# A chunked state-space scan and two feed-forward layers on one core: the first decays' broadcast, idle products, and the order of issue changed

## The chip, the cores and the metric

The kernel runs on one core of a Trainium2 chip. The metric is the time on the device in microseconds: the median of three executions, 371.07 us before the change (371.06 to 371.11). TensorE does the matrix products, VectorE and ScalarE work on rows, GpSimd (POOL) does a few small things, and SyncE (SP) issues nearly all DMAs.

## The reference: what is computed

There are three stages, on 4 sequences of 768 tokens, with 8 heads of 32 channels each and a state of 16. All of it is float32. Stage 1 is a scan with decay in chunks:

```python
for c in range(nc):
    cum = np.cumsum(log_a[:, :, sl], axis=-1)
    L = np.exp(cum[:, :, :, None] - cum[:, :, None, :]) * causal
    CB = np.einsum('bhin,bhjn->bhij', Cc, Bc)
    y_intra = np.einsum('bhij,bhjd->bhid', CB * L, xc)
    y_inter = np.einsum('bhin,bhnd->bhid', Cc, state) * np.exp(cum)[:, :, :, None]
    y[:, :, sl] = y_intra + y_inter
    state = decay_full * state + sum_j(B_j x_j * decay_from_j)
```

Stages 2 and 3 are feed-forward layers over 256 channels with 1024 hidden ones. Between them the tokens of a sequence are mixed through a matrix of rank 32:

```python
x = x + relu(layer_norm(x) * g @ w_ch1) @ w_ch2
u = x + (x.T @ U @ V).T
out = u + relu(u @ w21) @ w22
```

## The kernel before

**Tiles.** The tokens are worked in 24 chunks of 128, six to a sequence, in groups of 256 and 512 tokens (`GROUPS`). A chunk goes through the same steps: its operands are loaded (`xb`, `stk`), the decays are spread over all partitions (`bc`), a scan makes the decay matrix `lt` (line 707, VectorE), products make `cb` (lines 718, 723, TensorE), `mult` joins both into `mm` (lines 733, 736, VectorE), `bw` weights the input for the state (line 754), `sps` and `gst` carry the state on (lines 813, 831), and `yps` is the chunk's output (lines 771 to 798, TensorE). [...] It is also transposed (`tps`, line 888) for mean and variance.

**Feed-forward layers.** A group of tokens has eight hidden slices `f`. For each there is a group of six first products (`mm1`, `hps`, line 960), a high part by ScalarE (`hh`, line 967), a low part by VectorE (`hl`, line 971) and a group of second products (`mm2`, `acc`, lines 985 and 991). The first products of the first layer need centred weights: `pc` (line 401) multiplies each piece of `w1` by a centring matrix, and a closing product with `negi` (line 414) leaves the low part. The weights arrive as words of 64 bits; two ScalarE steps and a VectorE merge (`w`, line 381) make float32 of them, in three staging buffers (`raw`).

**The first four chunks' decays** don't go through DRAM. Eight rows are loaded into `r` (line 633), clipped, split into a high and a low part `rh` (lines 662, 272), and TensorE spreads them with a selection matrix `sel`:

```python
P.matmul(p, pair["sel"][:2 * ROWS, k, :], pair["h"][:, j, :], start=(j == 0), stop=(j == 1))
```

**The order.** The program is a list of items with an engine, a cost, predecessors and a due time. `Plan.issue` replays them by its own costs and at each step emits the item that is due first, so that the tables `FIRST`, `SHIFT`, `WARM` and the cost functions set the order on each engine. Every engine then runs its own list in order. `FIRST` lists items that go ahead of everything; `STAY` favours staying with feed-forward products once there (a bonus in the due time); `NEAR` lets an item wait a little for a better one. At most eight DMAs are under way, and SP's queue is in order.

**Idle products.** Where the plan sees TensorE without work early on, it emits products of zeros on zeros into a bank that nobody reads (`filler`, line 1145, tile `dummy`), as long as the next item is more than `WARM[3]` away. They wait for the tile `zero` (line 320), which VectorE sets first of all.

## Time and profile before

| | |
|---|---|
| median of three executions | 371.07 us |
| the profiled execution | 372.6 us |
| its span, first to last instruction | 370.7 us |
| mean granted clock of TensorE | 0.982 of full |
| PE busy | 361.2 us, 97% |
| DVE busy | 235.5 us, 64% |
| ACT busy | 169.9 us, 46% |
| POOL busy | 32.4 us, 9% |
| DMA bytes | 40.16 MB, mean 108 GB/s |

The page gives each engine's busy time and, below, its share in 40 slices of the span, in tenths (9 is 90% or more). [...] The view in order of time has start, length, engine, line, tile written from tiles read, and in brackets the idle time before it with what ended it. A product in float32 shows as two instructions. Lengths of products overlap, so the time that one costs is the distance between starts. The chain of waits follows the last instruction back to what released it, step by step.

### The profile page before, as it was taken

The page shows a single profiled execution, that of the slowest core. Times are in us where ns is not written, and L with a number is a line of the kernel's source. Part 1 is how long each engine was busy: PE and PEld are TensorE (multiplying, and loading weights), DVE is VectorE, ACT ScalarE, POOL GpSimd, SP SyncE. Part 2 cuts the span into 40 slices and gives each one's busy share as a digit, 9 for nine tenths or more (in the row PEclk, how much of TensorE's full clock was granted, in tenths as well). Part 3 has the DMA queues.
Part 4 walks back from the last instruction along what each step waited for, and adds up shares of the span by engine and source line. Part 5 has one row for each costly group of instructions (what it writes and reads, how often), then busy time and mean ns, then how long its engine had stood idle before and what let it go on. Part 6 is the DMA issues. An engine that isn't in the chain of part 4 may idle for free.

```text
span 370.7 us, 8298 instructions
## 1 busy us (share of the span) xinstructions
PE 361.2 (97%) x3297; PEld 306.8 (83%) x3297; DVE 235.5 (64%) x516; ACT 169.9 (46%) x475; POOL 32.4 (9%) x44
## 2 busy tenths in 40 slices
PE   6999899999999999999999999999999999999996
PEld 4677789879887789899887789989986789898895
DVE  5699889998627864884556794567626742343242
ACT  5488567886614651522424641233415552242231
POOL 3452744000002000000000000000000000000000
PEclk8599899999999999999999999999999999999999
DMA  7938636652002576780131505243011100000010
GB/s 216 275 110 281 173 108 204 205 167 87 6 17 88 202 293 197 221 282 1 57 94 44 198 3 184 71 150 129 9 35 44 38 21 0 2 0 30 1 58 28
DMA packets 29308, 40.16 MB, mean 108 GB/s; under 512 B 3806, under 2 KB 19214, under 8 KB 29270
## 3 DMA queue, kind: packets, MB, share of 16 engines
q1 hardware_dynamic: 28982, 39.46, 33.5%
q8 instruction: 26, 0.43, 0.5%
q10 hardware_dynamic: 288, 0.17, 0.2%
q14 instruction: 12, 0.10, 0.1%
HBM read 31.67 MB, written 7.95 MB: 107 GB/s over the span
## 4 chain that ended last, share of the span: by engine, by line
PE 84%; DVE 9%; DMA 4%; issue 1%; ACT 1%; SPq 0%; DVEq 0%
PE hps L960 33%; PE acc L991 19%; PE acc L985 15%; PE pc L401 2%; PE yps L777 2%; DMA xt<-in_xb 2%; PE cb L723 2%; PE ups L1072 1%; DMA raw<-in_w 1%; PE tps L888 1%; DVE hl L971 1%; DVE w L381 1%; PE yps L771 1%; PE cb L718 1%; PE yps L789 1%
## 5 line engine op out<-in xcount | busy, mean ns | idle before, releaser
L971 DVE SCALAR_TENSOR_TENSOR hl<-hps,hh 128x256 fp32r<-128x256 f32 (+1 forms) x128 | 70.5, 552 | 90.5 <-ACT hh L967 90.3
L967 ACT ACTIVATE hh<-hps 128x256 fp32r<-128x256 f32 (+1 forms) x128 | 62.7, 491 | 140.4 <-PE hps L960 137.7
L960 PE MATMUL hps<-yhl,w 128*128 128x512 f32 (+1 forms) x384 | 80.1, 344 | 0.1
L960 PE MATMUL hps<-uhl,w 128*128 128x256 f32 (+1 forms) x384 | 77.6, 338 | 0.0
L991 PE MATMUL acc<-hh,w 128*128 128x512 f32 (+1 forms) x256 | 74.4, 343 | 0.0
L985 PE MATMUL acc<-w,hh 128*128 128x256 f32 x384 | 73.5, 287 | 0.4 <-DVE w L272 0.4
L960 PEld LDWEIGHTS hps<-yhl,w 128*128 128x128 f32 x384 | 60.1, 193 | 8.5 <-issue 1.0
L960 PEld LDWEIGHTS hps<-uhl,w 128*128 128x128 f32 x384 | 60.8, 190 | 7.6 <-DVE uhl L272 0.3
L985 PEld LDWEIGHTS acc<-w,hh 128*128 128x128 f32 x384 | 62.2, 192 | 4.5 <-issue 1.0
L985 PE MATMUL acc<-w,hl 128*128 128x256 f32 x192 | 54.8, 285 | 0.0
L991 PEld LDWEIGHTS acc<-hh,w 128*128 128x128 f32 x256 | 46.0, 189 | 7.4 <-issue 1.2
L991 PE MATMUL acc<-hl,w 128*128 128x512 f32 (+1 forms) x128 | 43.1, 337 | 0.0
L707 DVE TENSOR_TENSOR_SCAN lt<-lt,eye 128x512 f32<-128x512 f32 x32 | 38.9, 1217 | 5.9 <-DMA lt<-arows 5.9
L985 PEld LDWEIGHTS acc<-w,hl 128*128 128x128 f32 x192 | 37.0, 193 | 0.0
L681 POOL TENSOR_SCALAR stp<-stp,parity 128x256 f32<-128x256 f32 x20 | 24.8, 1250 | 15.0 <-DMA stp<-in_cbT 14.9
L991 PEld LDWEIGHTS acc<-hl,w 128*128 128x128 f32 x128 | 24.2, 189 | 2.2
L736 DVE TENSOR_TENSOR mm<-cb,lt 128x512 f32<-128x512 f32 x24 | 15.6, 682 | 3.5 <-PE cb L723 3.5
L372 ACT ACTIVATE w<-raw 128x512 f32<-128x512 f32 (+2 forms) x19 | 12.2, 642 | 9.1 <-DVE w L272 3.7
L376 ACT ACTIVATE raw<-raw,half 128x512 int32<-128x512 uint16 (+2 forms) x19 | 13.9, 734 | 0.0
L269 ACT ACTIVATE yhl<-yps 128x128 fp32r<-128x128 f32 x48 | 11.1, 278 | 5.9 <-PE yps L777 3.0
L272 DVE TENSOR_TENSOR yhl<-yps,yhl 128x128 fp32r<-128x128 f32 x48 | 11.5, 282 | 3.0 <-ACT yhl L269 1.6
L269 ACT ACTIVATE yt<-tps 128x256 f32<-128x256 f32 x24 | 9.1, 378 | 9.2 <-PE tps L888 9.0
(110 smaller groups left out, 372.1 us busy)
## 6 DMA issues: line engine op xcount, KB each, us to landing
raw<-in_w SPq DMA_DIRECT2D x16, 512.0 KB, 5.4
lt<-arows SPq DMA_DIRECT2D x12, 512.0 KB, 4.6
stk<-st SPq DMA_DIRECT2D x48, 96.0 KB, 2.5
st<-sh SPq DMA_DIRECT2D x8, 384.0 KB, 6.8
xt<-in_xb SPq DMA_DIRECT2D x14, 192.0 KB, 3.6
lt<-arows SPq DMA_DIRECT2D x16, 128.0 KB, 4.0
out<-u SPq DMA_DIRECT2D x8, 256.0 KB, 2.1
xt<-in_xb SPq DMA_DIRECT2D x20, 96.0 KB, 3.4
```

Source lines behind the costliest of these rows:

```text
L269: A.activation(out=out, in_=in_, func=AF.Copy, **kw)
L272: eng.tensor_tensor(out=out, in0=in0, in1=in1, op=ALU.subtract)
L372: A.activation(out=cell["t"], in_=words(1).bitcast(F32), func=AF.Prelu, scale=2.0 ** -112, alpha=-2.0 ** 32)
L376: A.activation(out=words(0), in_=cell["r"][:rows, :2 * n].bitcast(U16).rearrange("p (n w) -> p n w", w=4)[:, :, 1], func=AF.Identity, scal ...
L681: eng.tensor_scalar(out=t[:, 2 + i], in0=t[:, 1], scalar1=m, scalar2=None, op0=ALU.mult)
L707: V.tensor_tensor_scan(t, pair[k] if k < ROWS else t, eye, 0.0, op0=ALU.mult, op1=ALU.add)
L736: V.tensor_tensor(out=mm_[k][:, s_], in0=cbp[k, hf], in1=lt[k][:, s_], op=ALU.mult)
L960: P.matmul(p[:, :n], w[:, k, fs], x[:, k, :], start=(i == 0), stop=(i == 5))
L967: A.activation(out=hh[:, :n], in_=hps[l, key, f][:, :n], func=AF.Relu)
L971: V.scalar_tensor_tensor(out=hl[:, :n], in0=hps[l, key, f][:, :n], scalar=0.0, in1=f32(hh[:, :n]), op0=ALU.max, op1=ALU.subtract)
L985: P.matmul(p, x[:, t * C:(t + 1) * C], w[:, f, :], start=(f == 0 and i == 0 and t % 2 == 0), stop=(f == NF - 1 and i == 2), skip_group_che ...
L991: P.matmul(accs[l, key][d][:, :n], w[:, f, ds_], x[:, :n], start=(f == 0 and i == 0), stop=(f == NF - 1 and i == 2))
```

## The change

It has four parts, and the new constants of the planner go with them.

- **Broadcast.** The tile `rh` has 128 rows, not 8. VectorE sets it to zero first (`bcz`, 1024 columns), then the eight rows are written as before, and the product contracts over all 128 rows of `sel` and `rh`.
- **Idle products.** Once a gap is found, idle products are emitted until the plan's time is 0.2 us past the moment at which the next item can start; before, until it was nearer than 0.3 us. There are 57 of them, not 29.
- **First loads.** `FIRST` names the first chunks' operands ahead of the weights. `cst0` goes to the end of that list, and so stands behind `ra` on ScalarE's queue.
- **Order.** New costs, shifts, `STAY` 2.65 for 1.24, `NEAR` 0.03 for 0, and an item that follows on its own engine counts no latency.

```diff
--- before.py
+++ after.py
@@ -22,14 +22,14 @@
 NF = DFF // 128
 GROUPS = ((0, 256), (256, 512))
 
-WARM = (1.2, 6.0, 28, 0.3)
+WARM = (1.1, 3.8, 28, 0.3)
 EARLIEST = {'warm': 30.0}
 NS = (2, 2, 1, 1)
 FINE = sum(n == 2 for n in NS)
 PARTS = ((0, 2), (2, NC))
 
-FIRST = [('bc0', 0), (('w1', 0, 0), 'ld'), 'cst', (('w1', 0, 1), 'ld'), ('stk', 2), 'rows', ('xb', 0), 'cst0',
-         ('stk', 0), ('ra', 0, 0), ('sel', 0), ('bcl', 0), (('w2', 0, 0), 'ld'), ('ra', 0, 2)]
+FIRST = [('bc0', 0), ('sel', 0), ('stk', 0), ('xb', 0), ('bcl', 0), ('stk', 2), 'cst', (('w1', 0, 0), 'ld'),
+         ('ra', 0, 0), 'rows', (('w1', 0, 1), 'ld'), (('w2', 0, 0), 'ld'), ('ra', 0, 2), 'cst0']
 
 ACTQ = ['cst0', ('ra', 0, 0)]
 
@@ -42,23 +42,23 @@
          "000 001 010 101 011 020 100 111 021 110 030 121 031 120 131 130".split()]
 
 
-LAT, PER, T0, NEAR, SWITCH, STAY = 0.287, 1, -5.78, 0, 0.056, 1.24
+LAT, PER, T0, NEAR, SWITCH, STAY = 0.287, 1, -6.36, 0.03, 0.056, 2.65
 dve = lambda n: 0.065 + n / 960
 scn = lambda n: 0.06 + n / 480
 dve2 = lambda n: 0.065 + n / 1920
 mmr = lambda n: (n + 32) / 2400
 act = lambda n: 0.093 + n / 1200
 actp = lambda n: 0.051 + n / 1200
-pool_tt = lambda n: 0.0024 * n
-sp = lambda n, kb, run: (ISSUE * n, kb / 16 * (0.04 / run + 1 / 36))
+pool_tt = lambda n: 0.0043 * n
+sp = lambda n, kb, run: (ISSUE * n, kb / 16 * (0.045 / run + 1 / 31))
 BLOCK, FETCH = 256, 5.8
 ISSUE, FLIGHT, BEGIN = 0.52, 8, 0.75
-SP_FIRST, SP_LAST = 0.65, 0.92
+SP_FIRST, SP_LAST = 0.4, 0.8
 FIRST_NEAR = 2.0
 
 
 
-SHIFT = dict(zip("rows w0 w1 w2 ra0 ra chunk0 chunk".split(), [-96.3, -27.2, -54.91, 17.22, -39.9, -41.6, -51.31, -1.1]))
+SHIFT = dict(zip("rows w0 w1 w2 ra0 ra chunk0 chunk".split(), [-3.25, -6.22, -22.15, 12.19, -25.03, -114.94, -21.66, 2.83]))
 
 
 def kind(n):
@@ -181,7 +181,8 @@
             it = items[n]
             if eng == "PE":
                 now = max(free[eng], WARM[0])
-                while n != "dummy" and now < WARM[2] and t - now > WARM[3]:
+                gap = t - now > WARM[3]
+                while n != "dummy" and now < WARM[2] and gap and t + 0.2 > now:
                     self.filler()
                     step = dict(words=2, cost=0.109 if now > WARM[1] else 0.216)
                     now = max(now, self.fetched(step))
@@ -220,7 +221,7 @@
             it["fn"]()
             left -= 1
             for m in succ[n]:
-                at[m] = max(at[m], end)
+                at[m] = max(at[m], free[eng] if items[m]["eng"] == eng and not it["dma"] else end)
                 wait[m] -= 1
                 if not wait[m]:
                     ready.setdefault(items[m]["eng"], set()).add(m)
@@ -636,7 +637,7 @@
 
             p = pair[k] = ps_m.tile([128, 512], F32, tag="m", name="bcp")
             for j in range(2):
-                P.matmul(p, pair["sel"][:2 * ROWS, k, :], pair["h"][:, j, :], start=(j == 0), stop=(j == 1))
+                P.matmul(p, pair["sel"][:, k, :], pair["h"][:, j, :], start=(j == 0), stop=(j == 1))
 
         def bcast():
             lt[k] = att_p.tile([128, 1024], F32, tag="lt", name="lt", bufs=3)
@@ -647,7 +648,9 @@
             if k == 0:
                 pair["r"] = y_p.tile([2 * ROWS, 512], F32, tag="uhl0", name="r2")
                 pair["sel"] = y_p.tile([128, ROWS, C], F32R, tag="uhl1", name="selr")
-                pair["h"] = y_p.tile([2 * ROWS, 2, 512], F32R, tag="yhl1", name="rh")
+                pair["h"] = y_p.tile([128, 2, 512], F32R, tag="yhl1", name="rh")
+                ours = pair["h"][:2 * ROWS]
+                add(("bcz", k), "DVE", 1.0, lambda: V.memset(f32(pair["h"]), 0.0), due=-3e3)
                 sl_ = pair["sel"].rearrange("p k (i t) -> p (k i) t", i=2)
                 for j in range(0, ROWS, 2):
 
@@ -659,8 +662,8 @@
                 add(("bc1", k), "DVE", dve2(512), lambda: clip(pair["r"]), [("bc0", k)])
                 add(("bc2", k), "DVE", 0.07, lambda: V.memset(
                     pair["r"].rearrange("p (h i) -> p h i", i=w_)[:, :, 0:1], 0.0), [("bc1", k)])
-                add(("bch", k), "DVE", dve2(512), lambda: V.tensor_copy(pair["h"][:, 0, :], pair["r"]), [("bc2", k)])
-                add(("bcl", k), "DVE", dve(512), lambda: sub(V, pair["h"][:, 1, :], pair["r"], f32(pair["h"][:, 0, :])),
+                add(("bch", k), "DVE", dve2(512), lambda: V.tensor_copy(ours[:, 0, :], pair["r"]), [("bc2", k), ("bcz", k)])
+                add(("bcl", k), "DVE", dve(512), lambda: sub(V, ours[:, 1, :], pair["r"], f32(ours[:, 0, :])),
                     [("bch", k)])
             add(("bc", k), "PE", 0.46, bcast_first, [("bcl", 0), ("sel", k)], ring="m", words=4)
         else:
```

On TensorE at the start, where the first broadcasts (`bcp`, from `rh` and `selr`) stand, this is the end of the first 20 idle products and what follows before:

```order
L1145 MATMUL dummy<-zero 128x256
L639 MATMUL bcp<-rh,selr 128x512 x6
L401 MATMUL pc<-w_138,gd 128x256
L401 MATMUL pc<-w_138,gm 128x256 x2
L401 MATMUL pc<-w_138,gd 128x256
L639 MATMUL bcp<-rh,selr 128x512 x2
L1145 LDWEIGHTS zero
L1145 MATMUL dummy<-zero 128x256
```

And now, behind 23 idle products:

```order
L1148 MATMUL dummy<-zero 128x256
L640 MATMUL bcp<-rh,selr 128x512 x6
L721 MATMUL cb<-stp 64x256 x8
L640 MATMUL bcp<-rh,selr 128x512 x2
L1148 LDWEIGHTS zero
L1148 MATMUL dummy<-zero 128x256
```

The centring of the first weight piece (`pc`) is gone from between the broadcasts, and `cb` of the first two chunks stands there; 15 idle products follow.

On TensorE a little later, this is the stretch from the second centring to the first two chunks' outputs (`yps`) before:

```order
L401 MATMUL pc<-w_194,gd 128x256
L401 MATMUL pc<-w_194,gm 128x256 x2
L401 MATMUL pc<-w_194,gd 128x256
L813 MATMUL sps<-xt_93,bw 32x64 x8
L718 MATMUL cb<-stp 64x256 x8
L813 MATMUL sps<-xt_93,bw 32x64 x8
L414 MATMUL pc<-w_211,negi 128x512
L718 MATMUL cb<-stp 64x256 x8
L789 MATMUL yps<-rcb,gst 32x64 x8
L798 MATMUL yps<-mm,xt_93 32x64 x16
```

And now, from those outputs on, behind 13 more idle products:

```order
L792 MATMUL yps<-rcb,gst 32x64 x8
L801 MATMUL yps<-mm,xt_93 32x64 x16
L792 MATMUL yps<-rcb,gst 32x64 x16
L801 MATMUL yps<-mm,xt_93 32x64 x16
L891 MATMUL tps<-cst,yc 128x128 x2
L402 MATMUL pc<-w_260,gd 128x256
L402 MATMUL pc<-w_260,gm 128x256 x2
L402 MATMUL pc<-w_260,gd 128x256
L402 MATMUL pc<-w_362,gd 128x256
L402 MATMUL pc<-w_362,gm 128x256 x2
L402 MATMUL pc<-w_362,gd 128x256
```

Both chunks' outputs moved ahead of the first two centrings, which now follow each other. Behind them come four groups of first products (`hps`) in a row, where two stood alone before. Up to the first product of 512 columns the new order has all eight groups of first and eight of second products of the first token group, and five pairs of transposes; the order before has eight, six and four there. Over the whole program TensorE goes from feed-forward products to others 40 times, not 58; behind that first product of 512 columns 35 times, not 52.

On SP, the first DMAs before (`r` holds the first decays, `raw` a weight piece, `stp` and `xt` the chunks' operands):

```order
L254 DMA r_99<-in_a_rows 8x512
L254 DMA raw_112<-in_w 128x2x512
L254 DMA cst<-in_consts 128x256
L254 DMA raw_126<-in_w 128x2x512
L254 DMA stp<-in_cbT 128x256 x2
L254 DMA rows<-in_a_rows 88x256
L254 DMA xt_93<-in_xb 64x2x384 x2
L254 DMA stp<-in_cbT 128x256 x2
```

And now:

```order
L255 DMA r_99<-in_a_rows 8x512
L255 DMA stp<-in_cbT 128x256 x2
L255 DMA xt_93<-in_xb 64x2x384 x2
L255 DMA stp<-in_cbT 128x256 x2
L255 DMA cst<-in_consts 128x256
L255 DMA raw_170<-in_w 128x2x512
L255 DMA rows<-in_a_rows 88x256
L255 DMA raw_187<-in_w 128x2x512
L255 DMA raw_202<-in_w 128x2x512
```

The operands of the first chunks moved ahead of the first weight piece, and `rows` behind it.

## Rows read from the trace of the kernel before

**Rows 1.** The page's slices for PE, then stretches of the whole core.
```profile
PE   6999899999999999999999999999999999999996
...
5.00:10.00 5.00, 2.80 (x10) 1.95 (x9) 3.17 (x6) 2.64 (x5) 0.30 (x2) 0.72 1.05 297
...
15.00:20.00 5.00, 5.00 (x59) 3.46 (x57) 2.10 (x5) 2.82 (x6) 0.00 (x0) 0.76 0.57 153
40.00:50.00 10.00, 9.57 (x177) 8.80 (x178) 9.06 (x21) 7.15 (x26) 6.96 (x7) 0.83 0.42 120
50.00:60.00 10.00, 10.00 (x69) 8.35 (x69) 9.87 (x27) 6.12 (x13) 5.01 (x4) 1.00 0.61 174
```

**Rows 2.** TensorE in order of time, 0 to 20 us.
```profile
1.05 3.65 PE L1145 MATMUL dummy<-zero 128*128 128x256 bf16 x20 [1.05 <-DVE zero L320]
4.63 1.66 PE L639 MATMUL bcp<-rh,selr 8*128 8x512 f32 x6
8.48 1.22 PE L401 MATMUL pc<-w,gd 128*128 128x256 f32 x2 [2.20 <-DVE w L381]
```

**Rows 3.** The same stretches view, half a microsecond each: the granted clock.
```profile
7.00:7.50 0.50, 0.00 (x0) 0.00 (x0) 0.50 (x2) 0.50 (x2) 0.00 (x0) 0.66 1.07 379
...
17.00:17.50 0.50, 0.50 (x2) 0.39 (x2) 0.00 (x0) 0.00 (x0) 0.00 (x0) 0.60 0.81 272
```

**Rows 4.** The stretch 20 to 41, and a piece of the chain of waits.
```profile
20.00:41.00 21.00, 18.39 (x394) 13.94 (x394) 19.12 (x47) 15.54 (x47) 11.23 (x12) 1.00 0.77 219
...
32.74 6.43 DMA xt<-in_xb
```

**Rows 5.** TensorE in order of time, 46 to 52 us.
```profile
46.50 0.65 PE L789 MATMUL yps<-rcb,gst 32*32 32x64 f32 x32
...
47.46 0.51 PE L985 MATMUL acc<-w,hh 128*128 128x256 f32 x2
...
48.28 0.88 PE L960 MATMUL hps<-yhl,w 128*128 128x256 f32 x6
49.00 0.40 PE L985 MATMUL acc<-w,hh 128*128 128x256 f32 x2
...
49.72 0.88 PE L960 MATMUL hps<-yhl,w 128*128 128x256 f32 x6
50.52 1.09 PE L718 MATMUL cb<-stp 64*64 64x256 f32 x16
51.55 0.74 PE L960 MATMUL hps<-yhl,w 128*128 128x512 f32 x2
```

**Rows 6.** VectorE in order of time, 0 to 50 us.
```profile
0.82 0.17 DVE L320 MEMSET zero<- 128x128 f32 x1 [0.82 <-PEq L1188]
2.46 0.77 DVE L467 TENSOR_SCALAR r<-r 8x512 f32<-8x512 f32 x1 [1.47 <-DMA r<-in_a_rows]
3.29 0.07 DVE L660 MEMSET r<- 8x8 f32 x1
...
8.35 1.22 DVE L707 TENSOR_TENSOR_SCAN lt<-bcp,eye 128x512 f32<-128x512 f32 x1
...
43.58 0.55 DVE L467 TENSOR_SCALAR ra<-ra 128x768 f32<-128x768 f32 x1
```

**Rows 7.** TensorE in order of time, 22 to 26 us; last, pieces of the chain of waits.
```profile
22.93 0.50 PE L1145 MATMUL dummy<-zero 128*128 128x256 bf16 x3
23.27 0.38 PE L888 MATMUL tps<-cst,yc 128*128 128x128 f32 x2
23.81 0.70 PE L401 MATMUL pc<-w,gd 128*128 128x256 f32 x2 [0.16 <-DVE yhl L272]
...
25.64 0.38 PE L888 MATMUL tps<-cst,yc 128*128 128x128 f32 x2
...
19.49 0.36 PE sps L813 x16
19.85 0.42 PE pc L414
```

## The prediction

> **What bounds the kernel now.** I read the stretches first, then the clock, then TensorE's order of time, since only the engine that is never idle sets the end. TensorE is busy in nearly every slice of the span, and from 50 us on all of the time; VectorE is as full there (9.87 of 10 us) [rows 1]. So an end that comes earlier must come from the first 50 us, or from TensorE doing the same products in less time. In the first 50 us three things are lost. TensorE runs 20 idle products, then broadcast products that contract over 8 rows, and then stands 2.20 us for the first converted weights [rows 2]. The granted clock drops to half at about 7.2 us and is back at about 17.3 [rows 3]; between lie weight centring, broadcasts and six more idle products. VectorE meanwhile has only 2.10 us of work in 15 to 20 [rows 1]: the first chunks' products stand behind the weights. Between 20 and 41 TensorE is busy for 18.39 of 21 us and stands for 2.61; the longest of it ends a DMA on which the chain stood for 6.43 us, for the fifth chunk's `x` [rows 4]. Then the clock is lost again: its mean over 40 to 50 is 0.83 [rows 1], so 0.17 x 10 = 1.7 us are lost. The page's execution took 372.6 us with a span of 370.7; the median is 371.07, 1.5 below it. I take differences in the span and subtract them from the median.

> I compare at a **marker**: TensorE's first product of 512 columns, at 51.55 [rows 5]. Both orders have done there all eight first products of the first group, six chunks and all four centrings.

> **The start.** The new memset stands ahead of `zero`, for which the idle products wait. VectorE memsets take 0.07 us for 8 columns and 0.17 for 128 [rows 6], 0.83 ns a column, so 1024 columns take 0.92; at the rate of the clip of 768 columns in 0.55 [rows 6] it would be 0.73. I take 0.92, from the same operation. TensorE starts at 1.05 [rows 2] + 0.92 = 1.97. What else is queued behind the memset on VectorE loses nothing: the clip of the first rows waits for its DMA to 2.46 [rows 6]. The constants, now behind the first decays on ScalarE's queue, are wanted only for the selectors ahead of the first broadcast. [...]

> An idle product takes (23.27 - 22.93)/3 = 0.11 at full clock [rows 7], so 0.22 at half. The 20 idle products took from 1.05 to 4.63 [rows 2]; all at full clock would be 2.2 us, all at half 4.4, so some 12.5 ran at half and the clock rose near 3.8, after 2.7 us of them. The changed kernel will have run only 1.8 us of them at that time. That work alone doesn't bring it back at once is seen from 8.48 on, where TensorE went on without a gap and the clock came only at 17.3 [rows 2, 3]. I therefore expect the rise late, near the 7.15 us at which the clock changed before. The 23 idle products end at 1.97 + 23 x 0.22 = 7.0; with a rise at 3.8, 8 of them at half, at 5.4.

> **The broadcasts.** A product of 512 columns costs by columns: six took 1.66 with 8 rows [rows 2], and I price 128 rows the same, at nothing more. The rows that are added hold zeros. What they may give is the clock, since the clock fell just behind the 8-row products; after the rise nothing idles TensorE now, as idle products fill each gap.

> **The first chunks ahead of weights.** Before the first weight piece SP and ScalarE now load 16 + 128 + 37 + 512 + 384 = 1077 KB. At 297 GB/s [rows 1] from about 1.7 these are in by 5.4, and the weight of 512 KB (with 128 KB of constants) by 7.5, before its merge is due (13). VectorE needs the chunk's operands at 5 and later, so DMA hides here.

> TensorE's path, with full clock from 7.15: six broadcasts to 8.4; `cb` 1.05 to 9.5; two broadcasts to 9.9; 15 idle products to 11.6; both `sps`, 0.36 each, to 12.3; 13 idle products to 13.7; two chunks' outputs, 0.96 (46.50 to 47.46) and three quarters of it, to 15.5; transposes, 0.38, to 15.9; two centrings of 1.83 (23.81 to 25.64) to 19.6; transposes, two closing products of 0.42 and `cb` (50.52 to 51.55) to 21.8; four groups of first products in a row, 4 x 0.72 (48.28 to 49.00), to 24.7 [rows 5, 7]. VectorE can follow: its broadcast is there at 7.6, two scans of 1.22 to 10.0 [rows 6], `bw` to 10.5, in time for `sps`.

> From there to the marker stand: `sps` four times (1.4), six idle products (0.7), two centrings (3.7), two closing products (0.8), four chunks' outputs (3.8), four groups of first products (2.9), eight of second products at 0.72, 49.00 to 49.72 (5.8), two `cb` (2.1), three pairs of transposes (1.1): 22.3. Ten switches between the two kinds add 0.9 (below). The marker comes at 24.7 + 23.2 = 47.9, **3.65** earlier. VectorE bounds it from the other side: before, it was idle for 1.83 us in 5 to 10, 2.90 in 15 to 20 and 1.88 in 20 to 41 [rows 1, 4], 6.6 in all, and now for 1.2 while it waits for the broadcast. It can be 5.4 ahead, no more. Done by the marker are two more groups of second products (2 x 0.72) and a pair of transposes (0.38): **1.8** more, 5.45 with the 3.65, so that the two engines bound it alike.

> **Fewer switches.** A group of second products right after a chunk's output takes 0.82 (47.46 to 48.28), between first products 0.72; one of first products ahead of `cb` 0.80 (49.72 to 50.52) in place of 0.72 [rows 5]. Behind the marker TensorE leaves the FFN 35 times, not 52. 17 round trips at 0.18 are 3.1 us; nothing is the other bound, as transposes that lead into a mix may switch freely. I take half: **1.5**.

> **What such a chain leaves out** are waits not seen on paper. I charge half of the 2.61 us for which TensorE stood between 20 and 41 [rows 4]: **1.3**. Sum: 3.65 + 1.8 + 1.5 - 1.3 = 5.65, so 371.07 - 5.65 = **365.4**.

> **Rivals.** *Early rise.* The clock is full at 3.8 as before. The idle products end 1.6 earlier, of which VectorE lets TensorE keep 1.2 (its wait for the broadcast): 364.2. Against it stands the shorter run of products before that point.

> *Operands late further on.* The weight pieces need staging buffers that VectorE frees; loads behind them on SP wait too. If the hole of 39 us returns, it costs the other half of 2.61 and 1.7 of clock, 3.0: 368.4. For it: this very thing happened [rows 4]; against it: with the first operands ahead of the weights, the two first centrings no longer hold up chunks.

> *The clock isn't held.* If 128 zero-filled rows and idle products don't keep it, TensorE goes from 7 to about 17 at half again. 28 idle products cost 3.1 more, and broadcasts, `cb` and `sps` 1.6: gain 5.65 - 4.7 = 0.95, 370.1. For it: the clock stayed low before from 8.48 on, with the engine busy; against it: those were partly 8-row products.

> *Slower: the lumps.* With 17 fewer switches chunk work comes in longer lumps, and first products bunch: four in a row need four banks and four results of ScalarE and VectorE. VectorE is full from 50 to 60 [rows 1], and a scan of 1.22 [rows 6] ahead of a result can make the next second product wait. The gain is used up at 5.65/35 = 0.16 us a lump; at 0.2 the kernel takes 372.4. Against it: TensorE doesn't wait in that stretch now, with VectorE as full.

> **Numbers.** Forecast 0.45, early rise 0.18, late operands 0.18, clock not held 0.10, slower 0.09. A measurement here tells about 0.2%, 0.7 us. The likeliest gives 365.4. Its own range is 363.6 to 366.9, by the switches (3.1 to nothing) and the memset (0.2 less). The range over the cases, 362.5 to 369.3, reaches from an early rise with all the switches past one late hole, and leaves out the clock not held and the lumps, 0.19. Faster 0.89, same 0.03, slower 0.08.

> **What would show it.** TensorE's first idle product near 2.0; granted clock full from about 7.2 without a break to 45; four groups of first products in a row near 22, the marker at 47 to 50; no VectorE stretch like 15 to 20 with 2.1 of 5 us; TensorE's waits behind the marker as few as now. A marker at 51 or later, or waits of TensorE behind it, would make the prediction wrong.

## The result, and the profile after

The changed kernel takes 368.2 us (median of 20 runs, 367.0 to 372.4), the kernel before 372.61 beside it (20 runs, 368.4 to 375.2; the three shown ahead of the prediction lay at 371.1). The ratio is 0.9912, with a 95% interval of 0.9884 to 0.9941: faster by 0.9%, where the forecast of 365.4 meant 1.5%. It compares means and leaves out the two longest runs of the kernel before (374.78 and 375.19), which count as slow; the two medians give 0.988. The range of 362.5 to 369.3 holds it, the likeliest case's own range of 363.6 to 366.9 does not. The profiled execution took 369.13 us, its span is 367.3 (before 370.7), the mean granted clock 0.999 (before 0.982).

The page of the changed kernel: TensorE's total, then the busy tenths of TensorE and of the DMA engines and the granted clock in 40 slices of 9.2 us.

```profile
PE 357.0 (97%) x3325; PEld 306.7 (83%) x3325; DVE 236.8 (64%) x517; ACT 170.8 (47%) x475; POOL 30.7 (8%) x44
...
PE   7799999999999999999999999999999999999996
...
PEclk9999999999999999999999999999999999999999
DMA  7879355731004666920423623033302100000010
```

The clock reads full in every slice, but its first record stands at 5.05 us. The 23 idle products took 3.85 us (2.12 to 5.97): up to 5.07 they start 0.21 us apart, from there on 0.11. In the kernel before they stand 0.21 apart where the record is 0.50 (13.5 to 14.8 us), so by that it was half until about 5.05. The view of stretches for the same four stretches as [rows 1]; a line has the stretch and its length in us, then busy time and number of instructions of PE, PEld (weight load of TensorE), DVE, ACT and POOL, then the granted clock of TensorE as a share of full, the share of the DMA engines' time, and GB/s:

```profile
5.00:10.00 5.00, 5.00 (x43) 3.48 (x42) 4.49 (x10) 1.95 (x6) 2.92 (x5) 1.00 0.88 243
15.00:20.00 5.00, 2.67 (x14) 2.38 (x14) 4.94 (x8) 3.25 (x12) 2.43 (x4) 1.00 0.81 247
40.00:50.00 10.00, 10.00 (x216) 7.78 (x208) 8.56 (x22) 7.77 (x32) 5.64 (x4) 1.00 0.53 157
50.00:60.00 10.00, 9.86 (x60) 8.58 (x59) 9.90 (x22) 6.33 (x13) 4.60 (x4) 1.00 0.70 224
```

VectorE's hole of 15 to 20 (2.10 of 5 us before) is filled with 4.94, and TensorE has one in its place: 2.67 of 5. In order of time, VectorE's first steps and some of TensorE's:

```profile
1.01 0.91 DVE L653 MEMSET rh<- 128x1024 f32 x1 [1.01 <-PEq L1191]
1.90 0.17 DVE L321 MEMSET zero<- 128x128 f32 x1
...
2.12 4.09 PE L1148 MATMUL dummy<-zero 128*128 128x256 bf16 x23 [2.12 <-DVE zero L321]
5.97 1.62 PE L640 MATMUL bcp<-rh,selr 128*128 128x512 f32 x6
7.52 1.09 PE L721 MATMUL cb<-stp 64*64 64x256 f32 x16
8.55 0.73 PE L640 MATMUL bcp<-rh,selr 128*128 128x512 f32 x2
9.12 1.81 PE L1148 MATMUL dummy<-zero 128*128 128x256 bf16 x15
10.87 0.65 PE L816 MATMUL sps<-xt,bw 128*32 128x64 f32 x32
11.45 1.59 PE L1148 MATMUL dummy<-zero 128*128 128x256 bf16 x13
12.97 0.43 PE L792 MATMUL yps<-rcb,gst 32*32 32x64 f32 x16
13.33 0.45 PE L801 MATMUL yps<-mm,xt 64*32 64x64 f32 x32
13.71 0.65 PE L792 MATMUL yps<-rcb,gst 32*32 32x64 f32 x32
14.29 0.46 PE L801 MATMUL yps<-mm,xt 64*32 64x64 f32 x32
17.33 0.38 PE L891 MATMUL tps<-cst,yc 128*128 128x128 f32 x2 [2.58 <-ACT yc L270]
...
47.97 1.42 PE L963 MATMUL hps<-yhl,w 128*128 128x512 f32 x5
```

Three things are to be seen. The marker came at 47.97 (forecast 47.9). Ahead of it stands a pause of 2.58 us at 14.75 that the prediction did not have; the view puts it down to ScalarE's `yc`, which was ready at 14.64. And from the marker to the end of the span it is 319.33 us, where before it was 370.7 - 51.55 = 319.15: nothing of what the prediction took off there has come. TensorE's waits from 48 us on (who waited for whom; us in total, times, longest; `yhl` is a chunk's output in a high and a low part), where the kernel before has none behind 52:

```profile
PE cb L726 <- DMA stk<-st: 0.7, 1, 0.7
PE acc L988 <- DVE hl L974: 0.6, 1, 0.6
PE hps L963 <- DVE yhl L273: 0.4, 1, 0.4
```

So two questions: what is the pause, and what ate the gain behind the marker.

### The profile page after: what moved, and what is told of

Read it like the earlier page. It is cut to its first block, busy times and chain, and to the rows that moved or that the text cites. A ratio compares the mean times of both kernels' runs of the same rounds, so it can differ in the third digit from the quotient of the medians.

```text
span 367.3 us, 8353 instructions
## 1 busy us (share of the span) xinstructions
PE 357.0 (97%) x3325; PEld 306.7 (83%) x3325; DVE 236.8 (64%) x517; ACT 170.8 (47%) x475; POOL 30.7 (8%) x44
## 4 chain that ended last, share of the span: by engine, by line
PE 84%; DVE 6%; DMA 5%; issue 2%; SPq 1%; ACT 1%; DVEq 0%
PE hps L963 33%; PE acc L994 18%; PE acc L988 14%; PE dummy L1148 2%; PE pc L402 2%; PE cb L726 2%; DMA lt<-arows 2%; PE yps L780 2%; PE ups L1075 2%; PE tps L891 2%; DMA ra<-in_a_rep 1%; PE cb L721 1%; DVE hl L974 1%; DMA stk<-st 1%; PE yps L792 1%
## 5 line engine op out<-in xcount | busy, mean ns | idle before, releaser
L963 PE MATMUL hps<-yhl,w 128*128 128x512 f32 (+1 forms) x384 | 74.4, 339 | 0.5 <-DVE yhl L273 0.4
L963 PE MATMUL hps<-uhl,w 128*128 128x256 f32 (+1 forms) x384 | 73.9, 337 | 0.0
L988 PE MATMUL acc<-w,hh 128*128 128x256 f32 x384 | 72.4, 285 | 0.0
L994 PE MATMUL acc<-hh,w 128*128 128x512 f32 (+1 forms) x256 | 72.0, 342 | 0.0
L963 PEld LDWEIGHTS hps<-yhl,w 128*128 128x128 f32 x384 | 58.8, 190 | 8.2 <-DVE yhl L273 0.9
L988 PEld LDWEIGHTS acc<-w,hh 128*128 128x128 f32 x384 | 61.3, 191 | 3.2 <-issue 1.0
L684 POOL TENSOR_SCALAR stp<-stp,parity 128x256 f32<-128x256 f32 x20 | 22.9, 1161 | 16.2 <-DMA stp<-in_cbT 16.2
L373 ACT ACTIVATE w<-raw 128x512 f32<-128x512 f32 (+2 forms) x19 | 12.3, 645 | 6.7 <-DMA raw<-in_w 3.0
L273 DVE TENSOR_TENSOR yhl<-yps,yhl 128x128 fp32r<-128x128 f32 x48 | 11.5, 282 | 5.4 <-ACT yc L270 5.1
L270 ACT ACTIVATE yt<-tps 128x256 f32<-128x256 f32 x24 | 9.1, 380 | 12.3 <-PE tps L891 12.1
```

Source lines behind the costliest of these rows:

```text
L270: A.activation(out=out, in_=in_, func=AF.Copy, **kw)
L273: eng.tensor_tensor(out=out, in0=in0, in1=in1, op=ALU.subtract)
L373: A.activation(out=cell["t"], in_=words(1).bitcast(F32), func=AF.Prelu, scale=2.0 ** -112, alpha=-2.0 ** 32)
L684: eng.tensor_scalar(out=t[:, 2 + i], in0=t[:, 1], scalar1=m, scalar2=None, op0=ALU.mult)
L963: P.matmul(p[:, :n], w[:, k, fs], x[:, k, :], start=(i == 0), stop=(i == 5))
L988: P.matmul(p, x[:, t * C:(t + 1) * C], w[:, f, :], start=(f == 0 and i == 0 and t % 2 == 0), stop=(f == NF - 1 and i == 2), skip_group_che ...
```

## The experiments

Twelve runs were made, in three sets of four; those of a set ran beside each other, each set on another chip, with the kernel before beside it (372.32, 372.27 and 371.9). "To the last" is the distance from the marker to the end of TensorE's last product, in the profiled execution; +36.5 stands for 36.5 us behind the marker. One kernel that stands in two sets gave 367.15 and 365.71, so medians of different sets that are less than 1.5 us apart say nothing. Within a set the executions of one kernel lie 1 to 8 us apart, so I read differences of 1 us and more.

| set, run | median us | ratio to before, 95% | pause, us | marker | to the last |
|---|---|---|---|---|---|
| kernel before | 372.61 | | none | 51.55 | 315.64 |
| changed kernel | 368.2 | 0.9912 [0.9884, 0.9941] | 2.58 | 47.97 | 315.81 |
| 1 broadcast over 8 rows | 368.94 | 0.9920 [0.9884, 0.9957] | none | 48.82 | 314.81 |
| 1 wide idle products | 367.05 | 0.9891 [0.9852, 0.9930] | none | 47.14 | 314.20 |
| 1 without 13 idle products | 367.15 | 0.9884 [0.9837, 0.9930] | none | 46.46 | 315.94 |
| 1 `zero` set first | 368.61 | 0.9929 [0.9896, 0.9963] | 3.49 | 50.30 | 315.46 |
| 2 changed kernel again | 368.61 | 0.9928 [0.9896, 0.9961] | 0.75 | 47.13 | 317.45 |
| 2 without 34 idle products | 367.15 | 0.9880 [0.9839, 0.9922] | none | 47.17 | 314.52 |
| 2 before, broadcast over 128 | 370.43 | 0.9962 [0.9929, 0.9995] | 0.56 | 47.68 | 317.41 |
| 2 new front, old rest | 369.87 | 0.9944 [0.9907, 0.9982] | 2.34 | 47.72 | 316.80 |
| 3 without 34, `xt` earlier | 365.89 | 0.9878 [0.9827, 0.9929] | none | 46.40 | 314.58 |
| 3 that, and a scan later | 365.18 | 0.9856 [0.9808, 0.9904] | none | 46.51 | 314.25 |
| 3 without 34 once more | 365.71 | 0.9862 [0.9817, 0.9908] | none | 46.03 | 314.44 |
| 3 without 34, 8 rows | 366.33 | 0.9886 [0.9832, 0.9939] | none | 46.38 | 314.43 |

**Broadcast over 8 rows.** My theory was that the clock had been won by the 128 rows; the rival was the order alone.

```diff
-P.matmul(p, pair["sel"][:, k, :], pair["h"][:, j, :], ...)
+P.matmul(p, pair["sel"][:2 * ROWS, k, :], pair["h"][:2 * ROWS, j, :], ...)
```

> The changed kernel with one thing undone: the eight broadcast products contract over the 8 rows that carry data; the memset of the 128-row tile, the order and all idle products stay. Clock theory (the early gain is owed to products that keep TensorE's clock up): the granted clock rises near 5 us as in the changed kernel, falls within some 4 us of the first 8-row product at 6.0, and comes back only after 12 us; the work up to 14.7 us runs partly at half speed, so the first 512-column product comes 1.5 to 4 us later than 47.97 and the run takes 368.5 to 371.5 us beside 367 to 369 for the changed kernel. Order theory (the gain is owed to the order of loads and of issue; the idle products alone hold the clock): the clock stays full from 5 us, first 512-column product within 0.3 us of 47.97, the time within 0.3 us.

The view of stretches of this run:

```profile
10.00:11.00 1.00, 1.00 (x6) 0.59 (x7) 1.00 (x4) 0.24 (x1) 0.95 (x2) 0.92 0.96 324
11.00:12.00 1.00, 1.00 (x7) 0.69 (x6) 1.00 (x4) 1.00 (x2) 0.00 (x0) 0.50 1.02 378
...
14.00:15.00 1.00, 1.00 (x32) 0.86 (x22) 0.67 (x3) 0.00 (x0) 0.00 (x0) 0.87 0.91 224
```

TensorE is busy all of the time, and the clock falls all the same, from 10.85 to 14.26: in this profile the clock theory holds. TensorE, slowed by this and by a rise at 7.43 in place of 5.05, came to the place of the pause at 17.7 and found nothing to wait for, so the marker is 0.85 later than in the changed kernel's profile, not 1.5 to 4. The median (368.94) lies near the changed kernel's (368.2, and 368.61 in the next set), but that doesn't make the fall free. Part the twelve runs by their mean granted clock, which counts from its first record on: six at 0.998 to 1.000 took 367.3 to 368.9 us, five at 0.994 or 0.995 took 369.0 to 371.4, and one at 0.991 took 373.3. So with 8 rows the clock falls in some runs and not in all, and a fall goes with some 2.4 us here.

**Fewer instructions.** The trace has a packet of 16384 bytes on an instruction queue (`q8`) that starts at 14.62. The DMA view of the stretches 10 to 14.6 and 14.6 to 16 (queue, kind: packets, MB, share of the 16 engines):

```profile
q1 hardware_dynamic: 954, 1.44, 100.4%
...
q1 hardware_dynamic: 209, 0.17, 51.6%
q8 instruction: 1, 0.02, 6.0%
```

My theory now was that TensorE had run out of instructions. Two ways of giving it fewer ahead of that point, with the order kept:

```diff
 wide idle products: each two of 256 columns become one of 512
+    calls[0] += 1
+    if calls[0] % 2:
+        P.matmul(dummy[0].rearrange("p (i n) -> p i n", i=2), zeros[:, :C], wide, ...)
 without 13 idle products
+    if not 38 < calls[0] <= 51:
         P.matmul(dummy[0][:, :256], zeros[:, :C], zeros, ...)
```

> The changed kernel with each two idle products of 256 columns made one of 512, so the same TensorE time in 28 fewer products and 56 fewer instructions up to 26 us. Code theory (TensorE's pause from 14.75 to 17.33 us is the wait for its next block of 256 instructions, whose 16 KB packet starts at 14.62; the block's end lies at the 449th instruction): the end of the block moves 50 instructions on, behind both centrings and the second pair of transposes; the pause ahead of the first transposes goes, the packet starts up to 2 us later, and the first 512-column product comes 1 to 2.5 us earlier, near 46: 365 to 367.5 us. Operand theory (the transposes waited for ScalarE's yc, as the waits list has it): the pause stays where it is and as long, 2.3 to 2.8 us, and the time within 0.4 us of the changed kernel.

> The changed kernel without the 13 idle products of 11.45 to 12.97 us (26 instructions); order kept. Code theory: the block ends 26 instructions on, inside the second weights' centring; the packet starts near 14.6 as before, TensorE goes on with transposes and 5 to 6 products of the centring from 14.75, and pauses there for at most 1 us until about 17.3; the first 512-column product 1 to 2.3 us earlier than 47.97, the time 365.5 to 367.5 us. Operand theory: the pause stays ahead of the transposes, 2.3 to 2.8 us. Clock: if 1.5 us without a product is enough to lose it, a fall of the granted clock between 11 and 20 us takes 1 to 4 us away again; if not, full from 5 us to the end.

In both the pause ahead of the transposes is gone. TensorE without the 13 products, in order of time:

```profile
14.28 0.46 PE L801 MATMUL yps<-mm,xt 64*32 64x64 f32 x32
14.66 0.44 PE L891 MATMUL tps<-cst,yc 128*128 128x128 f32 x2
15.65 0.70 PE L402 MATMUL pc<-w,gd 128*128 128x256 f32 x2 [0.55 <-DVE yhl L273]
```

The operand theory falls: the same `yc`, and no wait. What the code theory had wrong is a remaining pause at the new end of the block; TensorE came to its 220th product at 18.38, 3.6 us after the packet had started (14.74). With the wide products the marker came 0.8 earlier than in the changed kernel's profile, not 1 to 2.5.

**`zero` set first.** `zero`'s memset ahead of that of `rh`:

```diff
-add(("bcz", k), "DVE", 1.0, lambda: V.memset(f32(pair["h"]), 0.0), ...)
+add(("bcz", k), "DVE", 1.0, lambda: [V.memset(zero, 0.0), V.memset(f32(pair["h"]), 0.0)], ...)
```

> The changed kernel with VectorE's memset of the small zero tile ahead of that of the 128-row tile, so that idle products start 0.9 us earlier; TensorE's order the same. Early-clock theory (the clock rises a fixed while after TensorE's first product, 2.9 us in the changed kernel): first idle product near 1.2, rise near 4.1 us, idle products done near 5.5, but the broadcast still waits for its operand until 5.9, so the first 512-column product within 0.4 us of 47.97 and the time within 0.4 us. Rival (a gap of 0.4 us or more ahead of the broadcast lets the clock fall): a fall between 5 and 9 us, 1 to 3 us slower. Second rival (the rise does not follow the first product but falls where it falls): rise anywhere between 3.7 and 7.2.

The first idle product came at 1.05, the rise at 5.63, 0.6 later than in the changed kernel's profile: the rise does not follow the first product by a fixed time (the second rival). TensorE reached the pause 0.25 us earlier and stood 3.49 us, the clock fell behind it at 19.28, and the marker went to 50.30. An earlier start is worth nothing here.

**The changed kernel again; without all 34 later idle products; the 128 rows alone.** In the second the products behind the broadcast are left out (`calls[0] <= 23`). In the third the kernel before gets the tile of 128 rows, its memset ahead of the clip, and products over 128 rows:

```diff
-pair["h"] = y_p.tile([2 * ROWS, 2, 512], ...)
+pair["h"] = y_p.tile([128, 2, 512], ...)
-lambda: clip(pair["r"])
+lambda: [V.memset(f32(pair["h"]), 0.0), clip(pair["r"])]
-P.matmul(p, pair["sel"][:2 * ROWS, k, :], ...)
+P.matmul(p, pair["sel"][:, k, :], ...)
```

> The changed kernel once more, as the yardstick for the runs beside it and for a second profile. Every theory: 367 to 370 us. Code theory: if TensorE reaches the end of its second block of instructions (the 449th) before the packet that starts near 14.6 has landed, a pause of 2 to 3.5 us ahead of the first transposes; where a clock that rose late has slowed TensorE by then, a shorter one. Order theory of the rest (the waits behind the first 512-column product belong to the new order): the distance from it to TensorE's last product is 315 to 316 us, with single waits near +36.5, +160 and +198 us behind it.

> The changed kernel with the idle products kept only ahead of the broadcast (23 of 57); those in the gaps at 9.1, 11.5 and 25.9 us are left out, the order kept. Filler theory (products in the gaps keep the clock): TensorE is idle for 1.6 and 1.5 us between 9 and 13; the granted clock falls between 10 and 20 us for at least 3 us and the first 512-column product comes 1 to 3 us later than in the run without the 13 products (46.5), near 48 to 49.5: 367 to 370 us. Rival (the 128-row broadcast, cb, sps and yps between them are enough): the clock stays full, the block of instructions ends 56 instructions later so no pause ahead of the transposes, first 512-column product near 46 to 46.5: 365 to 367 us.

> The kernel before with nothing but the broadcast's contraction over 128 rows instead of 8 and the memset that this wants, put where VectorE is idle; its order and idle products kept. Clock theory: the fall at 7.16 that follows the 8-row products stays away or comes later, after the 2.2 us wait for the weights; if the clock is full from 7 to 17, the work of those 10 us (8 us of it TensorE's, bound also by VectorE's weights) shrinks by 1 to 3.5 us: 368.5 to 371 us beside 370 to 373 for the kernel before. Rival (the waits for the weights let the clock fall whatever the products): within 0.5 us of the kernel before and a fall between 7 and 12 as before.

The kernel before with 128 rows settled what the pause is. TensorE in order of time:

```profile
18.20 0.78 PE L790 MATMUL yps<-rcb,gst 32*32 32x64 f32 x32
18.91 0.42 PE L799 MATMUL yps<-mm,xt 64*32 64x64 f32 x23
19.90 0.32 PE L799 MATMUL yps<-mm,xt 64*32 64x64 f32 x9 [0.56 <-issue]
20.15 0.50 PE L1146 MATMUL dummy<-zero 128*128 128x256 bf16 x3
```

It stops in the middle of a chunk's output, where no operand changes. Add up the products ahead of it: 219. Add up those ahead of the pause in the changed kernel (23, 6, 16, 2, 15, 32, 13, 16, 32, 32, 32): 219 too. In all five profiles with a pause it stands at this count, and the product behind it starts 2.3 to 2.8 us after the packet does: 14.62 and 17.33, 12.95 and 15.51, 15.21 and 17.99, 14.47 and 17.11, 17.59 and 19.90. In the nine other profiles TensorE comes there 3.0 us or more after the packet's start, and there is no pause: in the kernel before at 22.7, with its packet at 19.42.

This run also shows that the 128 rows alone bring the old order's marker from 51.55 to 47.68, as early as the whole change does; in the profile its clock is full from 3.7 to the end, through a wait of 2.41 us for the weights. But only 1.8 us of that is left at the end: TensorE's `hps` then wait 1.9 us for VectorE's `yhl` near 75.

Without the 34 idle products the filler theory falls: TensorE is idle for 1.07 us in one piece, and the clock stays full in both profiles. It does not in every run: in 4 of this kernel's 12 the mean clock is 0.994 or 0.995, as in 4 of the changed kernel's 31 (0.993 to 0.995). Still the median is 1.5 us below the changed kernel's beside it. In the other profile of this kernel, in order of time:

```profile
9.92 0.71 PE L816 MATMUL sps<-xt,bw 128*32 128x64 f32 x32 [0.34 <-issue]
11.66 0.43 PE L792 MATMUL yps<-rcb,gst 32*32 32x64 f32 x16 [1.04 <-DVE gst L832]
...
13.69 0.44 PE L891 MATMUL tps<-cst,yc 128*128 128x128 f32 x2
```

And the changed kernel's second profile shows the other half of the story. Its pause was 0.75 us only, its marker 0.84 earlier; 4.6 us behind the marker TensorE stood for 2.16 us. VectorE and TensorE in order of time:

```profile
50.45 0.29 DVE L757 TENSOR_TENSOR bw<-xt,lt 128x128 f32<-128x128 f32 x1 [2.97 <-DMA xt<-in_xb]
...
53.12 0.69 DVE L974 SCALAR_TENSOR_TENSOR hl<-hps,hh 128x512 fp32r<-128x512 f32 x1
...
53.87 0.38 PE L988 MATMUL acc<-w,hl 128*128 128x256 f32 x1 [2.16 <-DVE hl L974]
```

VectorE waits for a chunk's `xt`, works off what hangs on it, and only then comes to the `hl` that TensorE wants. What TensorE had won, it waits out here.

**New front, old rest.** The lists of all engines as in the changed kernel up to the marker, from there as in the kernel before, without what is done already.

> The changed kernel's order of issue on every engine and queue up to the first 512-column product, and the order of the kernel before for all that is left from there. Rest theory (the new order of the rest saves switches but pays 2 to 3 us of new waits behind VectorE and DMA; the old one has about 1 us of waits): the distance from the first 512-column product to TensorE's last is 314 to 315 us, 0.5 to 2 us less than with the new order, and the waits at +36.5, +160 and +198 us are gone: 366 to 368.5 us. Rival (the new order of the rest is worth its 17 fewer changes of kind, and its waits come from the front, not the order): 316 to 318 us and 369 us or more. Third case: new waits at the seam, within 10 us of the first 512-column product, of more than 1 us.

316.80 to the last product, against 315.81 and 317.45 with the new rest: the old one is no better. The three named waits of the new order are gone, and others near +22 and +27 us (some 0.6, 0.9 and 0.9 us) are there. The rest theory as I put it is not borne out; the rival's figures came (316 to 318, and 369 or more). Either order gives back some of TensorE's lead, in waits for VectorE and for loads.

**Two waits taken on.** Both on top of the kernel without the 34 products. On SP's queue, then on VectorE:

```diff
+load xt, eighth chunk
 load lt, ninth chunk (two DMAs)
-load xt, eighth chunk

-scan of the twelfth chunk
 hl, fourth slice
+scan of the twelfth chunk
```

> The changed kernel without the 34 idle products behind the broadcast, and on SP's queue the two loads of the eighth chunk's xt moved ahead of the two loads of lt that stood before them; everything else as in the run without those 34. Load theory (behind the first 512-column product VectorE, and so TensorE, waits for xt, which lands at 48 to 50.5 us whenever TensorE comes there): xt is issued 1 to 2 us earlier, VectorE's wait ahead of its bw near 48 goes or shrinks under 0.4 us, TensorE's waits within 20 us behind the first 512-column product fall from 0.8 to under 0.4 us, the distance from there to the end 314.0 to 314.5: 366 to 367.2 us. Rival (lt is as late, its scan takes the wait over): a wait of VectorE for lt of 0.5 us or more in its place, no gain.

> The same, and on VectorE one scan of 1.22 us moved behind the second half hl that TensorE waited for at +36.5 us in all runs with the new order (0.74 to 1.06 us). Order theory of the rest: that wait goes, TensorE gains 0.6 to 0.8 us there, and keeps it if nothing else is late by the end: distance to the end 313.3 to 314 us, 365.3 to 366.6 us. Rival (VectorE is late as a whole, not by this scan): a wait of about the same length turns up within 10 us behind it, and the distance stays above 314.

> The changed kernel without the 34 idle products behind the broadcast, once more, as the yardstick beside the two above: 365 to 368 us, median near 367; clock full from 7 us or earlier; no pause ahead of the first transposes of over 0.6 us; distance from the first 512-column product to the end 314 to 316 us.

With `xt` issued earlier the rival's wait took its place:

```profile
46.20 1.23 DVE L707 TENSOR_TENSOR_SCAN lt<-lt,eye 128x512 f32<-128x512 f32 x1 [1.78 <-DMA lt<-arows]
```

The distance is 314.58 against 314.44 without the move: no gain, as the rival had it. With the scan moved too, the wait at +36.5, 0.50 to 0.86 us in the three profiles without the move, is 0.3 behind another of 0.3 ahead of its group, and one of some 0.7 stands at +159. TensorE's waits behind the marker (the lines are that kernel's own, three less):

```profile
PE acc L985 <- DVE hl L971: 0.6, 1, 0.6
PE hps L960 <- DVE yhl L270: 0.5, 1, 0.5
```

This fits a VectorE that is late as a whole and not by this scan, which no run here proves. 365.18 is the fastest median of the study, but 0.5 from its neighbour, which can't be told from none.

**Neither 128 rows nor idle products in the gaps.**

> The changed kernel with both clock measures undone that stand behind the first idle products: the broadcast over 8 rows, and no idle products in the gaps. Clock theory: the granted clock falls within some 4 us of the first 8-row product and, with TensorE idle for parts of 9 to 13 us, comes back only after 14 us; the work up to there is bound by loads and VectorE, so the first 512-column product comes at 48 to 50: 368 to 371 us. Rival (the new order alone, with its products of 128 rows close behind, holds the clock): full from about 7 us, first 512-column product near 47: 366.5 to 367.5 us.

```profile
11.00:13.00 2.00, 0.95 (x56) 0.75 (x56) 1.96 (x8) 1.41 (x3) 0.00 (x0) 0.95 1.02 347
13.00:15.00 2.00, 2.00 (x66) 1.44 (x59) 1.97 (x8) 2.00 (x8) 0.13 (x2) 0.50 0.88 210
```

The clock falls at 12.79 and is back at 16.20, as the clock theory has it, but the time is 366.33, 0.6 above that with 128 rows, which can't be told from none: near the rival's time, with the theory's clock. TensorE is busy while the clock is low (2.00 of 2 us from 13 to 15) and starts the first group of first products at 21.01, 0.62 later than with 128 rows (20.39). It loses no more because there it waits for VectorE in between (0.18 and 0.41 us near 14 and 16).

**A version that beats both.** The changed kernel without the 34 idle products behind the broadcast: 12 runs in two sets, 365.1 to 367.7, where the changed kernel never went under 367.0 in 31. In the five profiles without these products the marker comes at 46.0 to 47.2 and the distance to the last is 314.2 to 314.6, so the early marker is not given back there. What makes their distance shorter than the changed kernel's (315.81 and 317.45) is not shown.

## Why the prediction was wrong

**The start.** The memset took 0.91 us (0.92 forecast) and the first idle product came at 2.12 (1.97). The clock rose at 5.05 in both profiles of the changed kernel, between the early 3.8 and the late 7.15 that I took; in other kernels with the same start it rose at 5.1 to 7.4. The two chunks' outputs ended at 14.75, not at 15.5: 0.75 us gained.

**The pause.** The next step, transposes that the prediction has from 15.5 to 15.9, came at 17.33. The chain knew operands and engines, but nothing of the packet of 16384 bytes on the instruction queue that started at 14.62, 2.71 us ahead of that step. In the changed kernel many small products and 51 idle ones bring TensorE to its 219th product by 14.7; before it came there at 22.7, 3.3 us behind its packet (19.42), and didn't stop. The idle products that were to save the clock cost 1.5 us (368.61 against 367.15 in one set), and in both profiles without them the clock held.

**The marker.** 47.97 for 47.9 is in part luck: the pause made the first groups end 1.2 late (25.88 for 24.7), and the stretch from there to the marker took 22.1 us where I had 23.2. That the change would be 3.65 ahead at the marker is right.

**The step that failed** is what I set behind the marker: 1.8 for work done by then, 1.5 for switches, less 1.3 for unseen waits, in all 2.0 us. Measured: -0.18 in the first profile, -1.9 in the second (368.2 - 47.13 = 321.07 us against 319.15). Of the kernel before there is one profile, so how much its own distance varies is not known. By its terms, in the first profile:

- *Work.* 12 second products fewer at 0.12 are 1.44 us, as forecast; the 0.38 for a pair of transposes does not show (next item).
- *Switches.* Leaving the FFN costs 0.043 us on top of the product's usual distance (1.46 us in 34, and 2.22 in 52 before; a 35th stands under the waits), so 0.76 less. What chunk work and the way back take together is 48.7 us in either: nothing is saved there, since chunk pieces that now stand together change among themselves. 0.76, not 1.5: a quarter of the upper bound of 3.1.
- *Waits.* The places where a product comes over 0.14 us later than its kind's usual distance add up to 4.1 us, against 1.1 to 1.4 before, by how the usual distance is taken: 2.7 to 3.0 more, not 1.3. In the second profile they are some 4.9 more. That is the term that was most mis-sized.

1.44 + 0.76 - 3.0 gives -0.8, with 2.7 it is -0.5; the measured -0.18 leaves 0.3 to 0.6 unassigned, much of it in the 384 first products of 512 columns, which started about 1 ns closer to each other (every 0.229 us).

I had taken those waits as a share of the old ones between 20 and 41 us. In the profiles with the longest of them they belong to something else: TensorE's lead over VectorE and the loads. I did work out VectorE's bound ahead of the marker ("the two engines bound it alike"), and then let TensorE run on 2 us faster behind it, with VectorE busy 9.90 of 10 us.

**The rivals.** The time is that of late operands further on (368.4), and half of the mechanism too: no hole at 39 us, but waits for loads behind the marker, as in the second profile. The lumps came as described, with a scan of 1.22 us ahead of an `hl`. The changed kernel:

```profile
83.89 1.22 DVE L710 TENSOR_TENSOR_SCAN lt<-lt,eye 128x512 f32<-128x512 f32 x1
...
85.03 0.40 DVE L974 SCALAR_TENSOR_TENSOR hl<-hps,hh 128x256 fp32r<-128x256 f32 x1
...
85.49 0.39 PE L988 MATMUL acc<-w,hl 128*128 128x256 f32 x1 [0.58 <-DVE hl L974]
```

They cost some 3 us in all, not 7. The clock held in both profiles, so that rival is not the cause; but a fall was not free. The changed kernel's four runs with a mean clock of 0.993 to 0.995 took 369.8 to 371.3 us, and the median of the other 27 is 368.15. Where the clock was made to fall without idle products, the cost was not clear of noise (366.33 against 365.71). Early rise gained 0.75 at the outputs and nothing behind the pause.

**The signs** I named: the clock full without a break, the marker, no hole of VectorE, all came. "Waits of TensorE behind the marker as few as now" did not, and it was named as what would prove the forecast wrong.

## What to carry to other kernels

Ahead of an engine's work count its instructions too: here TensorE stood 0.56 to 3.49 us behind its 219th product in five profiles, and 51 of those 219 were idle ones in the changed kernel. With wide ones, or without 13 or 34 of them, no pause stood there; without the 34 the median was 1.5 us lower (367.15 against 368.61). A lead of TensorE was worth no more here than VectorE and the loads could follow (with 128 rows alone 3.87 us at the marker, 1.8 at the end): price what they lack at the point where the gain is to be cashed, not by the old waits. And price a fall of the clock in the stretch where it comes: in three kernels of the new order with idle products the runs with one were 2.1 to 2.6 us longer, and without the 34 idle products the difference was not clear of noise (0.6).

## What the runs showed of the hardware

Nor is it a matter of a kernel's start alone. TensorE's longest waits from 20 us on in the run with the wide idle products:

```profile
PE gps L1036 <- issue: 0.8, 1, 0.8
PE yps L801 <- issue: 0.5, 1, 0.5
```

They end at 73.65 and 38.26 us, at instructions 1986 and 962 by the count above: 449 and 6 or 2 times 256, to within one. Each time TensorE went on 2.4 to 3.1 us after the start of a packet of 16384 bytes. Two profiles without the 34 products (365.71 and 366.33) have a stop at instruction 1986 as well, 0.66 us at 73.07 and 0.35 at 72.87, which the view puts down to a tile of VectorE's (`vrq`) that the product doesn't read. None of the waits listed for the changed kernel stands at such a count.

**The clock with 8 and with 128 rows.** In the profile with products over 8 rows and TensorE busy throughout, the granted clock fell from 1.00 to 0.50 at 10.85 us; without the idle products, and with gaps, it fell at 12.79. With the same products over 128 rows, 120 of them zeros, it stayed at 1.00 in either kernel's profiles, and in the old order even through 2.41 us of waiting. It is a matter of how often: a mean clock of at most 0.995 stands in 6 of 12 runs with 8 rows and in 4 of 31 of the changed kernel; without the 34 idle products in 6 of 6 with 8 rows and 4 of 12 with 128; in the old order in 24 of 28 with 8 rows and 7 of 12 with 128. TensorE's busy time alone does not tell, as the run with 8 rows shows with 1.00 of 1.00 us busy and a clock of 0.50 (11 to 12 us), beside 1.00 busy and 1.00 in the changed kernel's same stretch.
